# Attention and the first layer's early products in the program's order on every engine, with the state products first and the state in two copies

## The chip, the core and the metric

The kernel runs on one core of one Trainium2 chip. The metric is device time in microseconds of one execution. The engines are TensorE (PE, with its weight loads as PEld), VectorE (DVE), ScalarE (ACT), GpSimd (POOL) and SyncE (SP), whose queue issues all transfers here. The kernel is built by a framework whose scheduler chooses the order of instructions on each engine from a simulated timeline, unless the program says otherwise; on the chip each engine then takes its instructions in that order.

## The reference

A retention layer (linear attention with a decay per head), then two dense feed-forward layers:

```python
for t in range(S):                       # S = 768, batch 2, 8 heads of 64
    state = gamma * state + einsum('bhd,bhe->bhde', k[:, :, t], v[:, :, t])
    y[:, :, t] = scale * einsum('bhd,bhde->bhe', q[:, :, t], state)
x = y as 1536 tokens of 512 features
g = mish(x @ w_in); x = g @ w_out                                  # d_ff 2048
x = (sigmoid(x @ w_gate) * (x @ w_val)) @ w_out2                   # d_ff 1536
```

## The kernel before

**Attention.** The 1536 tokens are 12 chunks of 128, six for each batch. For a chunk j, `at_scores` (line 432) makes the scores of all heads (tile `sc`, 8 matmuls on 64 rows of the array), POOL scales the values (`vp`) and, for the first chunks, prepares a scale table (`og`), and DVE masks the scores into `a`. `at_out` (line 450) adds up the chunk's output in tile `ao`: 8 matmuls of `a` with `vp` on 128 rows (line 457) and, except in the first chunk of a batch, 8 of the state with the queries on 64 rows (line 465). DVE scales it into `acc`. `at_state` (line 473) adds the chunk's keys and values to the state in PSUM (tile `st`, 8 matmuls on 128 rows, line 482), and ACT copies it into the one tile `s_t`, from which the next chunk's `at_out` reads. A chunk thus has four groups of 8 matmuls: scores, output, state read (I call it inter) and state.

**Transfers.** Each chunk loads two blocks of 512 KB (`qk_t`, `nv_t`, three buffers each). The weights come in pieces of 512 KB as 64-bit numbers (`raw`, three buffers) and are decoded to fp32: ACT (line 77, `v`), three DVE steps (lines 78 to 80), then `put` splits the result into a high part (ACT, line 67) and a low part (DVE, line 68) in `w`. `pump` (line 176) starts one such step of the weights.

**Dense products beside attention.** All dense products are three matmuls of 512 columns (hh, hl, lh), made by `mm3`. While attention runs, eight pieces of the first layer, each of 12 matmuls into one bank `h`, are made beside chunks 4 to 11 (line 519 and line 522): four for tokens 0 to 511, from `xc` (the split of `acc` by `put_plain` after chunk 3), and four for tokens 512 to 1023, from `B11` and `B21` (the split after chunk 7). ACT makes `e` (Mish) from each bank and `g`'s high part, POOL `g`'s low part. `blocks` (line 492) writes for each chunk j: scores of chunk j+1, one dense piece, output and state of chunk j, loads of chunk j+3.

**Order.** Scores, output, state and loads stand under `tc.high_priority()`; apart from that the scheduler chooses freely, so it mixes groups of matmuls, decode steps and transfers as its timeline sees fit.

**After attention.** `out1_first(0)` (line 535) begins the long dense part of 2244 matmuls, in which PE is the engine that sets the pace up to the end.

## Time and profile before

| | |
|---|---|
| median of 3 runs | 619.88 us (617.69 to 619.91) |
| the profiled execution's own time | 619.43 us |
| its span (first to last instruction) | 617.6 us |
| PE busy | 605.4 us (98%) |
| DVE, POOL, ACT busy | 412.5, 314.2, 250.3 us |
| `qk_t`, `nv_t`: issue to landing, median | 4.7, 5.5 us |
| `raw` of the first layer: issue to landing, median | 3.7 and 3.8 us |

PE is busy nearly all the time by this count, but a matmul that waits in the array for a change of shape counts as busy, so the busy share does not say how much of the time is work. The shares of the chain of waits and the duration of groups of matmuls say more. Attention and the eight dense pieces beside it end at about 95 us; the rest of the span is the dense part.

### The profile page before, as it was taken

Reading aid. Unit: us, or ns where it says so; the run is one execution under the profiler, and the core shown is the slowest. Engines: PE = TensorE matmul, PEld = TensorE weight load, DVE = VectorE, ACT = ScalarE, POOL = GpSimd, SP = SyncE. Lnnn points to the kernel's source line nnn. Section 1 sums busy time; section 2 is a strip of 40 time slices with the busy share of each in tenths; the row PEclk is TensorE's granted clock in tenths of the full one; section 3 lists DMA queues with packets and bytes.
Section 4 is the critical chain, followed back from the end, with each engine's and each line's share of the span. In section 5 each row is a group of like instructions: output and inputs, shape, how many; then the busy total and the mean of one; then the engine's idle time right before and its main releaser. Section 6 shows DMA issues by size and latency. Waiting matters only on the chain.

```text
span 617.6 us, 7968 instructions
## 1 busy us (share of the span) xinstructions
PE 605.4 (98%) x3056; PEld 488.7 (79%) x3056; DVE 412.5 (67%) x572; ACT 250.3 (41%) x433; POOL 314.2 (51%) x263
## 2 busy tenths in 40 slices
PE   8999999999999999998999999999999999999997
PEld 6767778888878788886788777888888888888885
DVE  3998339604795848647676996778477587573454
ACT  2535135624635444433443555543244244333210
POOL 5222333513968658546660556757378367466200
PEclk9999999999999999999999999999999999999999
DMA  9985301300321304121012012213112122100014
GB/s 342 370 319 169 120 2 36 102 2 34 103 88 50 136 1 137 52 85 68 34 36 69 0 64 73 70 68 102 34 69 68 69 68 76 61 1 1 1 51 154
DMA packets 15591, 52.27 MB, mean 85 GB/s; under 512 B 1984, under 2 KB 2112, under 8 KB 15552
## 3 DMA queue, kind: packets, MB, share of 16 engines
q1 hardware_dynamic: 15552, 51.75, 24.2%
q8 instruction: 24, 0.39, 0.3%
q14 instruction: 15, 0.12, 0.1%
HBM read 48.60 MB, written 3.15 MB: 84 GB/s over the span
## 4 chain that ended last, share of the span: by engine, by line
PE 76%; DVE 16%; POOL 3%; issue 2%; ACT 2%; DMA 1%; SPq 0%; DVEq 0%; ACTq 0%; POOLq 0%
PE h L86 31%; PE o L86 30%; PE hx L86 7%; DVE v L79 4%; DVE v L80 3%; DVE v L78 2%; PE ao L457 2%; PE sc L438 2%; DVE acc L324 2%; PE ao L465 2%; POOL w L68 1%; POOL g L68 1%; POOL og L444 1%; DVE T L68 1%; PE st L482 1%
## 5 line engine op out<-in xcount | busy, mean ns | idle before, releaser
L68 POOL TENSOR_TENSOR g<-e,g 128x512 fp32r<-128x512 f32 x80 | 115.0, 1445 | 120.9 <-ACT g L67 120.9
L86 PE MATMUL o<-g,w 128*128 128x512 f32 x576 | 141.3, 394 | 2.9 <-DVE acc L324 2.7
L86 PEld LDWEIGHTS o<-g,w 128*128 128x128 f32 x576 | 108.6, 190 | 28.2 <-DVE acc L324 5.0
L86 PE MATMUL h<-T,w 128*128 128x512 f32 x444 | 112.2, 390 | 1.0 <-DVE T L68 0.6
L68 POOL TENSOR_TENSOR w<-v,w 128x512 fp32r<-128x512 f32 x56 | 76.2, 1369 | 67.7 <-ACT w L67 67.5
L86 PE MATMUL o<-w,g 128*128 128x512 f32 x432 | 106.0, 389 | 0.0
L86 PE MATMUL h<-B,w 128*128 128x512 f32 x384 | 100.3, 391 | 0.8 <-DVE e L314 0.8
L86 PEld LDWEIGHTS h<-T,w 128*128 128x128 f32 x444 | 83.2, 188 | 19.4 <-DVE T L68 1.0
L86 PEld LDWEIGHTS o<-w,g 128*128 128x128 f32 x432 | 81.0, 188 | 17.1 <-POOL g L68 0.4
L86 PEld LDWEIGHTS h<-B,w 128*128 128x128 f32 x384 | 71.6, 188 | 16.7 <-DVE e L314 1.3
L324 DVE TENSOR_TENSOR acc<-o,acc 128x512 f32<-128x512 f32 x72 | 49.0, 685 | 39.0 <-PE o L86 38.7
L67 ACT ACTIVATE g<-e 128x512 fp32r<-128x512 f32 x84 | 52.5, 630 | 53.2 <-DVE e L314 35.1
L67 ACT ACTIVATE w<-v 128x512 fp32r<-128x512 f32 x68 | 42.4, 630 | 72.3 <-DVE v L80 44.4
L77 ACT ACTIVATE v<-raw 128x512 f32<-128x512 f32 x68 | 45.2, 670 | 57.8 <-POOL w L68 20.0
L86 PE MATMUL h<-xc,w 128*128 128x512 f32 x264 | 67.6, 393 | 0.1
L78 DVE TENSOR_SCALAR v<-v 128x512 int32<-128x512 int32 x68 | 51.1, 752 | 24.5 <-ACT v L77 24.2
L79 DVE SCALAR_TENSOR_TENSOR v<-raw,v 128x512 int32<-128x512 int32 x68 | 64.9, 955 | 1.3
L68 POOL TENSOR_TENSOR w<-s,w 128x512 fp32r<-128x512 f32 x34 | 48.2, 1425 | 34.4 <-ACT w L67 34.0
L80 DVE SCALAR_TENSOR_TENSOR v<-raw,v 128x512 int32<-128x512 int32 x68 | 64.4, 947 | 0.6
L344 DVE TENSOR_TENSOR acc<-o,acc 128x512 f32<-128x512 f32 x60 | 41.1, 686 | 30.8 <-PE o L86 30.4
L86 PEld LDWEIGHTS h<-xc,w 128*128 128x128 f32 x264 | 49.1, 188 | 11.1 <-DVE xc L68 0.8
L86 PE MATMUL hx<-xc,w 128*128 128x512 f32 x216 | 55.6, 389 | 0.0
(62 smaller groups left out, 551.1 us busy)
## 6 DMA issues: line engine op xcount, KB each, us to landing
raw<-w1i SPq DMA_DIRECT2D x16, 512.0 KB, 3.7
raw<-w1o SPq DMA_DIRECT2D x16, 512.0 KB, 3.8
qk_t<-qk SPq DMA_DIRECT2D x12, 512.0 KB, 4.7
nv_t<-nv SPq DMA_DIRECT2D x12, 512.0 KB, 5.5
raw<-w2g SPq DMA_DIRECT2D x12, 512.0 KB, 3.2
raw<-w2v SPq DMA_DIRECT2D x12, 512.0 KB, 3.4
raw<-w2o SPq DMA_DIRECT2D x12, 512.0 KB, 3.4
out<-acc SPq DMA_DIRECT2D x12, 256.0 KB, 2.0
```

What stands on the lines that cost most here:

```text
L67: nc.scalar.activation(out=hi, in_=raw, func=AF.Copy)
L68: eng.tensor_tensor(out=lo, in0=raw, in1=hi.bitcast(F32), op=ALU.subtract)
L77: nc.scalar.activation(out=v, in_=high.bitcast(F32), func=AF.Copy, scale=2.0 ** -112)
L78: nc.vector.tensor_scalar(out=b, in0=b, scalar1=3, scalar2=None, op0=ALU.logical_shift_left)
L79: nc.vector.scalar_tensor_tensor(out=b, in0=low, scalar=29, in1=b, op0=ALU.logical_shift_right, op1=ALU.bitwise_or)
L80: nc.vector.scalar_tensor_tensor(out=b, in0=high, scalar=SIGN, in1=b, op0=ALU.bitwise_and, op1=ALU.bitwise_or)
L86: nc.tensor.matmul(out=o, lhsT=w(a), rhs=x(b), start=first and n == 0, stop=last and n == 2, skip_group_check=more)
L324: nc.vector.tensor_tensor(out=acc, in0=o, in1=acc, op=ALU.add)
L344: nc.vector.tensor_tensor(out=acc, in0=o, in1=acc, op=ALU.add)
L438: nc.tensor.matmul(out=sc[e][:, p, :], lhsT=t[r, 1, p, :], rhs=t[r, 0, p, :])
L457: nc.tensor.matmul(out=o[D * e:D * e + D, p, :], lhsT=v[:, 2 * p + e, :], rhs=a[:, e, p, :], start=p == 0, stop=p == NP - 1 and not inter, ...
L465: nc.tensor.matmul(out=o[r, p, :], lhsT=s_t[r, p, :], rhs=t[r, 0, p, :], start=False, stop=p == NP - 1, skip_group_check=True,)
```

## The change

A wrapper `InOrder` stands in front of each engine and the transfer queue. As long as the list `early` is not empty (up to the end of attention), each instruction that is issued through it is told to stand after the one issued before it on the same engine, so the scheduler must keep the program's order there. After attention `early.clear()` gives the choice back. With that the program's own order is rewritten: `fin` makes the state products before the output; a chunk's output, state, loads and one piece of weights stand ahead of its dense piece; the low part of a weight (`late`) is issued one step later than its high part; weights are loaded one per chunk, two ahead of the first chunk where there were three; and the state gets a tile of its own per chunk from a pool with two buffers, where it was one tile.

```diff
+    class InOrder:
+        def __init__(self, engine):
+            self.engine, self.last = engine, None
+        def __getattr__(self, name):
+            call = getattr(self.engine, name)
+            if not early:
+                return call
+            def ordered(**kw):
+                with tc.issue_after(self.last) if self.last else nullcontext():
+                    i = call(**kw)
+                self.last = i.ins
+                return i
+            return ordered
+    pe, dve, act, pool, sync = [InOrder(e) for e in (nc.tensor, nc.vector, nc.scalar, nc.gpsimd, nc.sync)]
...
     def put(key, v):
         t = slot(key)
-        split(v, t[:, 0], t[:, 1], lo_eng["w"])
+        hi, lo = t[:, 0], t[:, 1]
+        act.activation(out=hi, in_=v, func=AF.Copy)
+        late.append(lambda: lo_eng["w"].tensor_tensor(out=lo, in0=v, in1=hi.bitcast(F32), op=ALU.subtract))
+        if not early:
+            late.pop(0)()
...
     def pump(n=1):
+        while late:
+            late.pop(0)()
...
-            nc.scalar.activation(out=s_t, in_=st, func=AF.Copy)
+            s_t[j + 1] = at.tile([P, NP, D], F32, tag="s", name="s")
+            act.activation(out=s_t[j + 1], in_=st, func=AF.Copy)
 
         def fin(j):
+            at_state(j)
             at_out(j)
-            at_state(j)
 
         def blocks(j0, dense):
 
             for j in range(j0, j0 + SPC):
                 if j + 1 < NSUB:
-                    with tc.high_priority():
-                        at_scores(j + 1)
+                    at_scores(j + 1)
+                fin(j)
+                load(j + 3)
+                load_piece()
                 if dense:
                     dense.pop(0)()
-                with tc.high_priority():
-                    fin(j)
-                    load(j + 3)
+                if j < SPC:
+                    pump()
             run(dense)
```

On PE, one chunk with a dense piece before (chunk 5, the chunk after it gives the scores; L438 is scores, L457 output, L465 inter, L86 dense):

```order
L438 MATMUL sc<-qk_t 128x128 x3
L457 MATMUL ao<-a,vp 64x128
L438 MATMUL sc<-qk_t 128x128 x2
L457 MATMUL ao<-a,vp 64x128 x4
L438 MATMUL sc<-qk_t 128x128
L457 MATMUL ao<-a,vp 64x128
L438 MATMUL sc<-qk_t 128x128
L457 MATMUL ao<-a,vp 64x128
L438 MATMUL sc<-qk_t 128x128
L457 MATMUL ao<-a,vp 64x128
L465 MATMUL ao<-qk_t,s_t 64x128 x8
L86 MATMUL h<-xc,w 128x512 x12
```

and such a chunk now, on the same engine (chunk 7; every early instruction has the wrapper's line):

```order
L65 MATMUL sc<-qk_t 128x128 x8
L65 MATMUL st<-vp,nv_t 64x64 x8
L65 MATMUL ao<-a,vp 64x128 x8
L65 MATMUL ao<-qk_t,s 64x128 x8
L65 MATMUL h<-xc,w 128x512 x12
```

The matmuls of two groups that alternated one by one now stand in groups of 8, and the state products stand second.

On DVE, where chunk 3 ends and `xc` is made, before (L447 masks scores, L469 scales the output, L78 to L80 decode):

```order
L447 TENSOR_TENSOR a<-sc,ma 128x512 x2
L80 SCALAR_TENSOR_TENSOR v<-raw,v 128x512
L469 TENSOR_TENSOR acc_87<-ao,og_108 128x4x128
L78 TENSOR_SCALAR v<-v 128x512
L68 TENSOR_TENSOR w<-v,w 128x512
L79 SCALAR_TENSOR_TENSOR v<-raw,v 128x512
L68 TENSOR_TENSOR xc<-acc_87,xc 128x512 x2
L80 SCALAR_TENSOR_TENSOR v<-raw,v 128x512
L68 TENSOR_TENSOR xc<-acc_87,xc 128x512
```

and at the same place on DVE now:

```order
L65 TENSOR_TENSOR a<-sc,ma 128x512 x2
L65 TENSOR_TENSOR acc_87<-ao,og_108 128x4x128
L65 TENSOR_TENSOR w<-v,w 128x512
L65 TENSOR_SCALAR v<-v 128x512
L65 SCALAR_TENSOR_TENSOR v<-raw,v 128x512 x2
L65 TENSOR_TENSOR xc<-acc_87,xc 128x512 x4
L65 TENSOR_TENSOR a<-sc,ma 128x512 x2
```

The whole decode of the fourth piece now stands ahead of the first `xc`, and all four `xc` stand ahead of the next masking.

On ACT, where chunk 7 ends and `B11` and `B21` (here B_84 and B_85) are made, before:

```order
L77 ACTIVATE v<-raw 128x512 x2
L486 ACTIVATE s_t<-st 128x256
L67 ACTIVATE B_84<-acc_88 128x512 x2
L67 ACTIVATE B_85<-acc_88 128x512 x2
L308 ACTIVATE e<-h 128x512
L67 ACTIVATE w<-v 128x512
L67 ACTIVATE g<-e 128x512
```

and now:

```order
L65 ACTIVATE s<-st 128x256
L65 ACTIVATE e<-h 128x512
L65 ACTIVATE g<-e 128x512
L65 ACTIVATE v<-raw 128x512
L65 ACTIVATE w<-v 128x512
L65 ACTIVATE B_84<-acc_88 128x512 x2
L65 ACTIVATE B_85<-acc_88 128x512 x2
```

The four splits now stand behind the Mish of the dense piece just made, and behind a whole decode. From `out1_first` on, the order on PE is the same in both but for one group of six matmuls.

## Rows read from the trace of the kernel before

**Rows 1.** The page, part 4: shares of the chain that ended last.
```profile
PE 76%; DVE 16%; POOL 3%; issue 2%; ACT 2%; DMA 1%; SPq 0%; DVEq 0%; ACTq 0%; POOLq 0%
```

**Rows 2.** Table by stretch: length, busy us (instructions) of each engine, clock, DMA.
```profile
7.30:30.30 23.00, 21.10 (x308) 16.99 (x306) 20.18 (x33) 9.66 (x18) 10.46 (x10) 1.00 0.99 385
...
95.00:617.00 522.00, 513.63 (x2245) 421.11 (x2243) 350.68 (x477) 217.04 (x372) 283.12 (x233) 1.00 0.18 61
```

**Rows 3.** The same for 30.30 to 94.80, by tile: sc, ao, st, h.
```profile
30.30:94.80 64.50, 16.02 (x96) 10.87 (x96) 9.46 (x14) 1.00 0.43 149
...
30.30:94.80 64.50, 24.32 (x208) 14.08 (x208) 5.48 (x8) 1.00 0.43 149
...
30.30:94.80 64.50, 5.68 (x84) 3.92 (x80) 2.28 (x6) 1.00 0.43 149
...
30.30:94.80 64.50, 24.82 (x96) 17.16 (x96) 0.00 (x0) 3.54 (x6) 1.00 0.43 149
```

**Rows 4.** Chain of waits in order of time: start, us, piece (two records a matmul).
```profile
44.10 0.41 PE sc L438 x2
44.52 0.36 PE ao L457 x2
...
57.09 2.96 PE h L86 x12
...
81.44 1.09 PE sc L438 x16
82.53 1.02 PE ao L465 x16
83.55 0.61 PE st L482 x16
```

**Rows 5.** Timeline, ACT and DVE in the first chunks: start, us, what, [idle before].
```profile
13.20 0.69 ACT L77 ACTIVATE v<-raw 128x512 f32<-128x512 f32 x1 [4.03 <-DMA raw<-w1i]
...
17.65 0.42 DVE L78 TENSOR_SCALAR v<-v 128x512 int32<-128x512 int32 x1
17.99 0.68 DVE L68 TENSOR_TENSOR w<-v,w 128x512 fp32r<-128x512 f32 x1
...
18.59 0.68 DVE L80 SCALAR_TENSOR_TENSOR v<-raw,v 128x512 int32<-128x512 int32 x1
...
19.80 1.28 DVE L447 TENSOR_TENSOR a<-sc,ma 128x512 f32<-128x512 f32 x2
...
20.99 0.68 DVE L80 SCALAR_TENSOR_TENSOR v<-raw,v 128x512 int32<-128x512 int32 x1
```

**Rows 6.** Timeline: POOL and DVE at the same time.
```profile
23.60 1.11 POOL L440 TENSOR_TENSOR vp<-nv_t,ck 128x512 f32<-128x512 f32 x1 [2.79 <-DMA nv_t<-nv]
23.85 1.41 DVE L79 SCALAR_TENSOR_TENSOR v<-raw,v 128x512 int32<-128x512 int32 x1
```

**Rows 7.** Timeline: the first split, the first dense piece, the first of out1_first.
```profile
27.71 2.18 ACT L67 ACTIVATE xc<-acc 128x512 fp32r<-128x512 f32 x4
...
30.33 3.14 PE L86 MATMUL h<-xc,w 128*128 128x512 f32 x10
...
95.00 5.60 PE L86 MATMUL o<-g,w 128*128 128x512 f32 x24
```

**Rows 8.** Timeline: the split of a bank, high part on ACT and low part on POOL.
```profile
81.93 0.63 ACT L67 ACTIVATE g<-e 128x512 fp32r<-128x512 f32 x1
82.63 1.27 POOL L68 TENSOR_TENSOR g<-e,g 128x512 fp32r<-128x512 f32 x1 [4.22 <-ACT g L67]
```

**Rows 9.** Two waits of PE, and the clock by stretch around the second.
```profile
18.37 1.16 PE L438 MATMUL sc<-qk_t 64*128 64x128 f32 x16 [1.47 <-DMA qk_t<-qk]
...
290.56 9.74 PE L86 MATMUL o<-g,w 128*128 128x512 f32 x35 [2.29 <-DVE acc L324]
...
290.40:293.80 3.40, 3.24 (x8) 2.56 (x9) 0.98 (x3) 0.90 (x2) 0.85 (x1) 0.50 0.41 146
```

**Rows 10.** The page, part 6: a chunk's second block from issue to landing.
```profile
nv_t<-nv SPq DMA_DIRECT2D x12, 512.0 KB, 5.5
```

More of the change, by code (lines that the diff above doesn't have):

```diff
@@ L1 @@
-from contextlib import ExitStack
+from contextlib import ExitStack, nullcontext
 import numpy as np
@@ L75, in decode @@
         b = v.bitcast(I32)
-        nc.scalar.activation(out=v, in_=high.bitcast(F32), func=AF.Copy, scale=2.0 ** -112)
-        nc.vector.tensor_scalar(out=b, in0=b, scalar1=3, scalar2=None, op0=ALU.logical_shift_left)
-        nc.vector.scalar_tensor_tensor(out=b, in0=low, scalar=29, in1=b, op0=ALU.logical_shift_right, op1=ALU.bitwise_or)
-        nc.vector.scalar_tensor_tensor(out=b, in0=high, scalar=SIGN, in1=b, op0=ALU.bitwise_and, op1=ALU.bitwise_or)
+        act.activation(out=v, in_=high.bitcast(F32), func=AF.Copy, scale=2.0 ** -112)
+        dve.tensor_scalar(out=b, in0=b, scalar1=3, scalar2=None, op0=ALU.logical_shift_left)
+        dve.scalar_tensor_tensor(out=b, in0=low, scalar=29, in1=b, op0=ALU.logical_shift_right, op1=ALU.bitwise_or)
+        dve.scalar_tensor_tensor(out=b, in0=high, scalar=SIGN, in1=b, op0=ALU.bitwise_and, op1=ALU.bitwise_or)
         return v
@@ L85, in mm3 @@
         for n, (a, b) in enumerate(((0, 0), (0, 1), (1, 0))):
-            nc.tensor.matmul(out=o, lhsT=w(a), rhs=x(b), start=first and n == 0, stop=last and n == 2,
+            pe.matmul(out=o, lhsT=w(a), rhs=x(b), start=first and n == 0, stop=last and n == 2,
                              skip_group_check=more)
@@ L103 @@
     cnt = {"dma": 0, "raw": 0, "task": 0}
-    steps, sums_t, vs = [], {}, {}
-    lo_eng = {"w": nc.vector, "g": nc.gpsimd}
+    steps, late, sums_t, vs = [], [], {}, {}
+    lo_eng = {"w": dve, "g": pool}
     def load_piece():
@@ L112, in load_piece @@
         t = stg.tile([P, DM], I64, tag="raw", name="raw")
-        nc.sync.dma_start(out=t, in_=src[kind][i])
+        sync.dma_start(out=t, in_=src[kind][i])
         raws.append(t)
@@ L121, in next_raw @@
         cnt["raw"] += 1
-        while cnt["dma"] < min(len(pieces), cnt["raw"] + STG):
+        while not early and cnt["dma"] < min(len(pieces), cnt["raw"] + STG):
             load_piece()
@@ L188, in weight @@
             steps.pop(0)[1]()
+        while late:
+            late.pop(0)()
         return w_t[key]
@@ L222, in put_t4 @@
         for k in range(2):
-            split(ts[2 + k], b_t["T4"][:, k, 0], b_t["T4"][:, k, 1], nc.vector)
+            split(ts[2 + k], b_t["T4"][:, k, 0], b_t["T4"][:, k, 1], dve)
     g_t = {}
@@ L247, in p1 @@
             r["s1"] = up.tile([P, N], F32, tag="u", name="s1")
-            nc.scalar.activation(out=r["s1"], in_=r["b1"], func=AF.Copy)
+            act.activation(out=r["s1"], in_=r["b1"], func=AF.Copy)
         def p6():
@@ L270, in c22 @@
         def c22():
-            nc.vector.tensor_tensor(out=r["b2"], in0=r["bB"], in1=r["u3"], op=ALU.add)
+            dve.tensor_tensor(out=r["b2"], in0=r["bB"], in1=r["u3"], op=ALU.add)
         def p2():
@@ L307, in mish @@
         e = ep.tile([P, N], F32, tag="e", name="e")
-        nc.scalar.activation(out=e, in_=h, func=AF.Mish)
+        act.activation(out=e, in_=h, func=AF.Mish)
         put_g(e, key)
@@ L323, in o1 @@
         acc = acc_t[c][:, d, :]
-        nc.vector.tensor_tensor(out=acc, in0=o, in1=acc, op=ALU.add)
+        dve.tensor_tensor(out=acc, in0=o, in1=acc, op=ALU.add)
     def o1_first(c, d):
@@ L437, in at_scores @@
                     r = slice(D * e, D * e + D)
-                    nc.tensor.matmul(out=sc[e][:, p, :], lhsT=t[r, 1, p, :], rhs=t[r, 0, p, :])
+                    pe.matmul(out=sc[e][:, p, :], lhsT=t[r, 1, p, :], rhs=t[r, 0, p, :])
             vp_t[j] = at.tile([P, 2 * NP, D], F32, tag="vp", name="vp")
-            nc.gpsimd.tensor_tensor(
+            pool.tensor_tensor(
                 out=vp_t[j], in0=nv_t[j][:, 1], in1=ck[:, j % SPB].to_broadcast([P, 2 * NP, D]), op=ALU.mult
@@ L456, in at_out @@
                 for e in range(2):
-                    nc.tensor.matmul(
+                    pe.matmul(
                         out=o[D * e:D * e + D, p, :], lhsT=v[:, 2 * p + e, :], rhs=a[:, e, p, :],
@@ L464, in at_out @@
                         r = slice(D * e, D * e + D)
-                        nc.tensor.matmul(
-                            out=o[r, p, :], lhsT=s_t[r, p, :], rhs=t[r, 0, p, :], start=False, stop=p == NP - 1,
+                        pe.matmul(
+                            out=o[r, p, :], lhsT=s[r, p, :], rhs=t[r, 0, p, :], start=False, stop=p == NP - 1,
                             skip_group_check=True,
                         )
-            nc.vector.tensor_tensor(
+            dve.tensor_tensor(
                 out=acc_t[j // SPC][:, :, j % SPC * P:j % SPC * P + P], in0=o, in1=og[j % SPB], op=ALU.mult
@@ L481, in at_state @@
                 for e in range(2):
-                    nc.tensor.matmul(
+                    pe.matmul(
                         out=st[D * e:D * e + D, p, :], lhsT=k[:, 0, 2 * p + e, :], rhs=v[:, 2 * p + e, :],
@@ L515 @@
         load_piece()
+        load_piece()
         at_scores(0)
-        blocks(0, seq([lambda: None] * SPC))
+        blocks(0, [])
         put_plain()
```

73 lines of the change are left out of this document (37 added, 36 removed).

## The prediction

> **What bounds the kernel now.** I read the chain of waits by engine first: PE holds 76% of it and DVE 16% [rows 1]. Then the table by stretch. From 95 us to the end PE is busy 513.6 of 522 us [rows 2], and by the order PE does there what it did before, so whatever is gained or lost ahead of `out1_first` is handed on to the end. Its first matmul starts at 95.00 us [rows 7]; this is the time to forecast. Ahead of it lie two stretches. Up to about 30 us DVE is busy 20.2 of 23 us [rows 2]: it masks, scales and decodes, and the first dense piece, which waits for the split `xc`, starts at 30.33 [rows 7]. From there to 95 us the chain runs through PE alone, and the reader should look at how long a group of 8 matmuls takes there. Where scores and outputs alternate, a matmul of the one takes 0.41 us and one of the other 0.36; in one piece 8 scores take 1.09 us, 8 matmuls of `ao` 1.02, 8 of the state 0.61, and a dense piece of 12 with the change of shape behind it 2.96 [rows 4]. So 16 alternating matmuls cost 8 x 0.77 = 6.2 us against 2.1 in two groups: each change between 64 and 128 rows stops the array.
>
> **The change, part by part.**
>
> *Grouping.* By records (two a matmul for the fp32 groups), the stretch from the first dense piece to `out1_first` holds 96/16 = 6 groups of scores, 208/16 = 13 of output and inter, 80/16 = 5 of state (by the weight loads; some matmul records are doubtful) and 96/12 = 8 dense pieces [rows 3]. In the new order the same work stands behind the start of the first dense piece: scores of chunks 6 to 11, output of 5 to 11, inter of 5 and 7 to 11, state of 6 to 10. In groups it costs 6 x 1.09 + 13 x 1.02 + 5 x 0.61 + 8 x 2.96 = 6.5 + 13.3 + 3.1 + 23.7 = 46.5 us, where it took 95.00 - 30.33 = 64.7. **Gain: 18.1 us**, less what waits are new.
>
> *The start of the first dense piece.* Now DVE takes everything in the program's order: the decode of pieces 0 to 3 whole, maskings of chunks 2 to 4, outputs 1 to 3, low parts 0 to 2, then `xc`. It can begin when piece 0 has landed, and ACT's copy of it, at 13.20, ends at 13.9 [rows 5]; the queue carries the same bytes ahead of it. From the starts in rows 5, a decode takes 0.34 + 2 x 0.60 = 1.55, a pair of maskings 1.19, any other step 0.60. So 13.9 + 4 x 1.55 + 3 x 1.19 + 6 x 0.60 = 27.3; then ACT's high part of piece 3 (0.63) and of the first `xc` (2.18/4 = 0.55 [rows 7]): 28.5 at best. Against that, a DVE step that begins while POOL works can be held: a decode step of 0.68 took 1.41 and ended after POOL's `vp` [rows 5, 6]. POOL has `vp` and `og` in each of these chunks, so I bound it by 4 x 0.73 = 2.9: 31.4. I take 30.4, above the middle because handovers between engines are not counted: 0.1 later than now. Ends: -1.8 and +1.1. Cover: transfers. One weight piece less stands ahead of chunk 3's blocks, so the wait of 1.47 us for them [rows 9] should not grow.
>
> *The first dense piece itself.* Its twelve matmuls want the four parts of `xc` one after the other. ACT gives a high part each 0.55 us, DVE a low part each 0.60, so it takes about 0.4 us more than its own time. PE stands idle ahead of it: chunk 4's groups end when its masking (about 25 us in the same reckoning) is two groups old, near 27.5. The idle stretch is 2 to 3 us. Such a wait is in the trace: after 2.29 us PE ran 3.40 us at 0.50, that is 1.2 GHz instead of 2.4, and after 1.47 us it stayed at full clock [rows 2, 9]. Half of 3.4 us is 1.7 at most, and part of it falls on time in which PE would wait for `xc` anyway: I take 0.8 for both, between 0.4 and 2.1.
>
> The Trainium skill ("TensorE: Matmul & The Clock Gate", section "HAM oscillation — how this bites in real kernels") says that waits between bursts of matmuls bring the half rate back, burst after burst. By that rule a strict order, in which PE stands still more often but for shorter times, speaks against this change; by the rows only this wait is as long as the one that was followed by half clock, and the sum has 0.8 us for it. What the rule would make of all chunks is the third rival.
>
> *The second handover, at chunk 8.* `B11` and `B21` now stand on ACT behind the Mish of the piece just made, its split, and a whole decode. From the end of that piece: two ACT steps of 0.63 [rows 8], the copy 0.69 and the decode 1.55 [rows 5], the high part 0.63, then high parts at 0.55 each and a low part: the last at 4.1 + 4 x 0.55 + 0.68 = 7.0 us. PE meanwhile has scores, state, output and inter (1.09 + 0.61 + 2 x 1.02 = 3.7) and nine of its twelve matmuls (about 2.1), and would want that part at 5.9. So +1.1 at least; with two DVE steps held by POOL +2.6. I take 1.9.
>
> *The other chunks.* Here the new order could close a loop: masking of chunk j+2 stands on DVE behind the decode in chunk j, which is behind ACT's copy, which is behind the Mish of dense piece j. From the end of piece j this is 0.63 + 0.63 + 0.69 + 1.55 + 1.19 = 4.7 us; with POOL's low part and `vp` (1.27 and 1.11 [rows 6, 8]) both in the way 7.1. PE wants the masking one chunk and two groups later: 1.09 + 0.61 + 2 x 1.02 + 2.96, then 1.09 + 0.61, in all 8.4. Slack 1.3 to 3.7: nothing is lost. If the cover fails, I bound it by 0.3 in each of six chunks, 1.8. State first: the copy of the state has a chunk to be made, and with two tiles it no longer waits for the readers; it was not on the chain in groups, so I put it at nothing. Transfers: a chunk's blocks are issued after its buffer's last reader, 5.5 us before they land [rows 10], and are wanted a dense piece and a chunk later (2.96 + 6.7 us): hidden by 4 us. The queue holds a weight piece behind them and waits for the decode of the chunk before, which is over by then.
>
> *After attention* the order is kept, the waits there hang on PE, and everything moves by the same amount: 0. What is late next is the split of chunk 11's output, wanted 5.4 us after `out1_first` starts; DVE has about twelve steps of 0.60 from the end of inter 11, 2.7 us ahead: just in time.
>
> *Sum.* 18.1 - 0.1 - 0.8 - 1.9 = 15.3 us. `out1_first` at 79.7, and against the profiled execution's 619.43 us: **604.1 us**. That execution stands 0.45 below the median of the runs, which changes nothing.
>
> **The rivals.**
>
> *The handovers eat half of it.* Everything at its far end: start +1.1, first piece 2.1, second handover 2.6 and a half clock behind it 1.7, chunks 1.8: 9.3 of the 18.1 us, gain 8.8, 610.6 us. For it: DVE is nearly full up to 30 us. Against it: several independent terms must all go wrong.
>
> *The change does not do what it says.* If the long alternating stretches were long because a matmul waited for data, and not for the change of rows, grouping would only move the waits: 619.5 us. For it: nothing but that PE's busy time hides waits. Against it: the same groups take 1.09, 1.02 and 0.61 us when they stand alone [rows 4].
>
> *Slower: the loop of the order closes.* If a piece of weights lands late, ACT stands at its copy, DVE at its decode, and the masking and so PE behind both, in every chunk; before, the scheduler could put the masking ahead. From 3.7 us of delay on PE waits. If PE waited 2.3 us in each of the seven chunks and ran 3.4 us at half clock each time, as at 290 us [rows 9], a chunk would cost 2.3 + 1.7 = 4.0 more, 28 us in all: 632 us. It turns slower from 15.3/7 = 2.2 us a chunk. Against it: pieces are issued two chunks ahead, some 13 us. The page of the skill named above stands on this rival's side.
>
> **How the numbers follow.** My forecast (600.5 to 608) has 0.72; handovers that eat half (608 to 613) 0.14; no effect 0.05; slower 0.06; and 0.03 for a gain beyond 19 us, were the first dense piece 1.8 us earlier and nothing else lost. A range from 600.5 to 611 leaves out no more than 2 in 10. A measurement of this kernel tells about 0.5%, 3.1 us, from no change. Faster by more: 0.72 + 0.14 + 0.03 less a little, 0.88; within it 0.06; slower 0.06.
>
> **What would show it.** Right: in the new chain of waits every group of scores stands in one piece of about 1.1 us, `out1_first` starts near 80 us, PE waits for `xc` near 28 us and for `B11` at chunk 8, nowhere else over 1 us up to the end. The gain in the span equals that of `out1_first`. Wrong: PE waits for maskings (DVE) in chunks 5 to 11, granted clock at 0.50 between 40 and 75 us, groups of 16 records that take 2 us or more, or a dense part that is longer than the 522 us it took.

## The result: 609.6 us, and the profile after

The changed kernel takes 609.6 us in the median of 4 runs (609.13 to 611.22), the kernel before 619.26 us beside it: a ratio of 0.9852, with an interval of 0.9824 to 0.9881, so it is faster by 1.5%. The forecast was 604.1 us with a range from 600.5 to 611. The time lies inside the range, but at its slow end: by the prediction's own bands it belongs to the rival in which the handovers eat half of the gain (608 to 613, worked out as 610.6 us, chance 0.14) and not to the forecast (600.5 to 608, chance 0.72). The profiled execution took 610.06 us, with a span of 608.3.

`out1_first` now starts at 85.60 us, where it was 95.00 [rows 7]: 9.4 us earlier. The span is 9.3 us shorter. What was gained ahead of `out1_first` is handed on whole, as expected.

The table by stretch: length, busy us (instructions) of PE, PEld, DVE, ACT, POOL, then the granted clock. First three short stretches after waits, then the dense rest:

```profile
18.20:21.60 3.40, 3.40 (x40) 3.07 (x40) 3.33 (x5) 1.03 (x3) 3.04 (x2) 0.50 0.90 355
35.30:38.70 3.40, 3.40 (x13) 2.36 (x13) 2.86 (x5) 0.60 (x2) 0.00 (x0) 0.50 0.48 188
62.60:66.00 3.40, 3.14 (x7) 2.21 (x8) 3.16 (x6) 2.04 (x5) 0.00 (x0) 0.50 0.83 334
86.00:608.00 522.00, 513.37 (x2243) 420.73 (x2242) 354.48 (x482) 218.97 (x376) 292.78 (x233) 1.00 0.19 62
```

The last row is the twin of the second of [rows 2]: 513.4 busy of 522 us, where it was 513.6. From the first matmul of `out1_first` to the end it is 522.7 us, where it was 522.6. The first three are new: three times ahead of 86 us TensorE ran 3.4 us at 0.50, that is 1.2 GHz instead of 2.4. The kernel before had none there.

The same table by tile, from the first dense piece to `out1_first`, as in [rows 3] (sc, ao, h; PE first, then PEld):

```profile
33.29:85.70 52.41, 7.30 (x96) 6.15 (x96) 8.96 (x14) 0.93 0.48 169
...
33.29:85.70 52.41, 13.69 (x208) 11.25 (x208) 5.44 (x8) 0.93 0.48 169
...
33.29:85.70 52.41, 27.20 (x96) 19.01 (x96) 0.00 (x0) 4.17 (x7) 0.93 0.48 169
```

The counts are those of before, so the same work stands behind the first dense piece. The six groups of scores keep PE busy for 7.3 us instead of 16.0, the thirteen of output and inter 13.7 instead of 24.3. The dense pieces went up, from 24.8 to 27.2, because two of them run at half clock for the most part.

One chunk in the chain of waits (start, us, piece), the twin of [rows 4]:

```profile
49.97 1.09 PE sc L65 x16
51.06 0.61 PE st L65 x16
51.68 1.90 PE ao L65 x32
53.58 2.96 PE h L65 x12
```

Four whole groups, 6.56 us a chunk, and no wait between them.

The first handover in the timeline (start, us, engine, what, [idle before <- releaser]):

```profile
17.08 1.16 PE L65 MATMUL sc<-qk_t 64*128 64x128 f32 x16 [2.92 <-DMA qk_t<-qk]
...
23.20 1.49 POOL L65 TENSOR_TENSOR og<-og,sg 128x512 f32<-128x512 f32 x1
23.71 1.26 DVE L65 TENSOR_SCALAR v<-v 128x512 int32<-128x512 int32 x1
...
27.37 1.16 PE L65 MATMUL sc<-qk_t 64*128 64x128 f32 x16 [1.43 <-DMA qk_t<-qk]
...
28.77 1.29 POOL L65 TENSOR_TENSOR vp<-nv_t,ck 128x512 f32<-128x512 f32 x1 [4.08 <-DMA nv_t<-nv]
29.19 2.86 DVE L65 SCALAR_TENSOR_TENSOR v<-raw,v 128x512 int32<-128x512 int32 x2
30.02 1.48 POOL L65 TENSOR_TENSOR og<-og,sg 128x512 f32<-128x512 f32 x1
...
33.29 0.50 PE L65 MATMUL h<-xc,w 128*128 128x512 f32 x1 [2.24 <-ACT xc L65]
34.01 4.02 PE L65 MATMUL h<-xc,w 128*128 128x512 f32 x11 [0.23 <-DVE xc L65]
37.96 1.49 PE L65 MATMUL sc<-qk_t 64*128 64x128 f32 x16
```

The first dense piece starts at 33.29 us (before 30.33, [rows 7]) and is over at 37.96, after 4.67 us instead of 2.96. Two DVE decode steps that stand beside POOL's `vp` and `og` take 2.86 us instead of 1.42, one step 1.26 instead of 0.42. In the kernel before POOL had made all five `og` in one go, from 7.06 to 12.09 us, ahead of the decodes; the strict order puts one of them into each chunk, beside a decode.

The second handover, at chunk 8:

```profile
58.43 1.03 DVE L65 TENSOR_SCALAR v<-v 128x512 int32<-128x512 int32 x1 [0.49 <-ACT v L65]
59.49 2.14 DVE L65 SCALAR_TENSOR_TENSOR v<-raw,v 128x512 int32<-128x512 int32 x2
62.20 2.17 ACT L65 ACTIVATE B<-acc 128x512 fp32r<-128x512 f32 x4
62.86 4.63 PE L65 MATMUL h<-B,w 128*128 128x512 f32 x12 [2.74 <-ACT B L65]
...
67.43 1.16 PE L65 MATMUL sc<-qk_t 64*128 64x128 f32 x16
```

PE waits 2.74 us for `B11`, whose split stands on ACT behind a decode that takes DVE 3.2 us (58.43 to 61.63) beside POOL's steps, and the piece then runs at half clock, 4.63 us long. The chunk takes 10.97 us (scores at 56.45 and again at 67.42) instead of 6.56: 4.4 us lost.

### The profile page after: what moved, and what is told of

Its sections match the earlier page's. It is cut to its first block, busy times and chain, and to the rows that moved or that the text cites. A ratio compares the mean times of both kernels' runs of the same rounds, so it can differ in the third digit from the quotient of the medians.

```text
span 608.3 us, 7961 instructions
## 1 busy us (share of the span) xinstructions
PE 587.5 (97%) x3056; PEld 480.6 (79%) x3056; DVE 420.3 (69%) x572; ACT 249.8 (41%) x433; POOL 325.2 (53%) x263
## 4 chain that ended last, share of the span: by engine, by line
PE 74%; DVE 16%; DMA 2%; ACT 2%; POOL 2%; issue 2%; SPq 0%; DVEq 0%; ACTq 0%
PE o L108 31%; PE h L108 28%; PE hx L108 7%; PE h L65 4%; DVE v L101 3%; PE ao L65 2%; DVE v L102 2%; DVE v L100 2%; DVE acc L354 2%; DMA qk_t<-qk 2%; DVE v L65 1%; PE sc L65 1%; POOL w L162 1%; POOL g L90 1%; DVE T L90 1%
## 5 line engine op out<-in xcount | busy, mean ns | idle before, releaser
L90 POOL TENSOR_TENSOR g<-e,g 128x512 fp32r<-128x512 f32 x72 | 103.1, 1441 | 83.4 <-ACT g L89 83.4
L108 PE MATMUL h<-B,w 128*128 128x512 f32 x336 | 87.8, 390 | 0.8 <-DVE e L344 0.8
L108 PEld LDWEIGHTS h<-B,w 128*128 128x128 f32 x336 | 62.9, 188 | 14.4 <-DVE e L344 1.2
L89 ACT ACTIVATE g<-e 128x512 fp32r<-128x512 f32 x76 | 47.6, 631 | 52.6 <-DVE e L344 35.1
L161 ACT ACTIVATE w<-v 128x512 fp32r<-128x512 f32 x58 | 36.1, 630 | 62.6 <-DVE v L102 34.7
L100 DVE TENSOR_SCALAR v<-v 128x512 int32<-128x512 int32 x58 | 44.4, 767 | 23.2 <-ACT v L99 22.9
L99 ACT ACTIVATE v<-raw 128x512 f32<-128x512 f32 x58 | 38.6, 670 | 49.7 <-POOL w L162 20.0
L102 DVE SCALAR_TENSOR_TENSOR v<-raw,v 128x512 int32<-128x512 int32 x58 | 57.0, 984 | 0.5
L101 DVE SCALAR_TENSOR_TENSOR v<-raw,v 128x512 int32<-128x512 int32 x58 | 56.4, 973 | 1.1
L108 PE MATMUL h<-xc,w 128*128 128x512 f32 x216 | 54.8, 389 | 0.0
L108 PEld LDWEIGHTS hx<-xc,w 128*128 128x128 f32 x216 | 40.6, 188 | 8.4
```

The source lines that it names most:

```text
L89: act.activation(out=hi, in_=raw, func=AF.Copy)
L90: eng.tensor_tensor(out=lo, in0=raw, in1=hi.bitcast(F32), op=ALU.subtract)
L99: act.activation(out=v, in_=high.bitcast(F32), func=AF.Copy, scale=2.0 ** -112)
L100: dve.tensor_scalar(out=b, in0=b, scalar1=3, scalar2=None, op0=ALU.logical_shift_left)
L101: dve.scalar_tensor_tensor(out=b, in0=low, scalar=29, in1=b, op0=ALU.logical_shift_right, op1=ALU.bitwise_or)
L102: dve.scalar_tensor_tensor(out=b, in0=high, scalar=SIGN, in1=b, op0=ALU.bitwise_and, op1=ALU.bitwise_or)
```

## The experiments

The theory, once the result was known: the groups of matmuls bring what the sum said, and the shortfall sits in the two handovers, in new waits of PE and in the half clock that follows them. The rivals: the groups alone are worth less; or the loss is spread over all chunks; or another part of the change (the forced order, the state in two copies) costs it. Each ratio is against the kernel before, run in turn with it on the same chip; its medians there were 618.1 to 618.9 us.

| kernel | median us | ratio [interval] | first dense piece | out1_first |
|---|---|---|---|---|
| the change | 609.6 | 0.9852 [0.9824, 0.9881] | 33.29 | 85.60 |
| alternating groups | 636.0 | 1.0261 [1.0204, 1.0319] | 39.76 | 111.08 |
| no order forced | 606.0 | 0.9789 [0.9768, 0.9810] | 31.64 | 82.03 |
| before, without priorities | 611.4 | 0.9884 [0.9869, 0.9898] | 28.67 | 87.47 |
| order forced on PE alone | 614.2 | 0.9927 [0.9908, 0.9945] | 40.13 | 90.01 |
| on PE and the transfer queue | 606.6 | 0.9805 [0.9783, 0.9827] | 36.12 | 83.46 |
| state as before | 609.8 | 0.9851 [0.9832, 0.9869] | 33.58 | 85.13 |
| splits first | 605.6 | 0.9798 [0.9773, 0.9822] | 30.77 | 80.71 |
| splits first, no decode behind | 601.3 | 0.9705 [0.9678, 0.9732] | 31.01 | 76.67 |
| `og` first | 608.1 | 0.9819 [0.9795, 0.9843] | 32.88 | 83.63 |
| idle matmuls in the waits | 607.1 | 0.9817 [0.9782, 0.9851] | 36.72 | 85.90 |
| both splits and `og` first | 599.7 | 0.9689 [0.9669, 0.9709] | 34.77 | 80.44 |
| the same with idle matmuls | 598.0 | 0.9680 [0.9655, 0.9706] | 29.55 | 75.20 |

The last two columns come from each kernel's one profiled execution. For several kernels that was the longest of their runs; it is far from the median for the idle matmuls (610.36 us) and for both splits and `og` first (604.8 us), and 1.0 us from it for splits first with no decode behind (602.35 us).

### The grouping undone

```diff
-                    at_scores(j + 1)
+                    at_scores(j + 1, out_begin(j) if j >= SPC else None)
```

Here each score matmul is followed by one output matmul of the chunk before, from chunk 4 on (`out_begin` returns the function that makes one). All else of the change stays, the forced order too.

> The changed kernel, with one thing undone: in chunks 4 to 10 the 8 scores of the next chunk and the 8 output matmuls (128 rows) of this chunk alternate one by one again, in a forced order on PE. Theory (changes between 64 and 128 rows cost the time): 7 chunks x (6.2 - 2.0) = 29 us more PE time; a part of it falls into the waits at the two handovers (some 5 us), so about 634 us, slower than the kernel before. Rival (the groups were long because matmuls waited for data): no more than 1 us a chunk, about 610 us.

It took 636.0 us, 2 us above the theory's value, and slower than the kernel before. The total is in part luck, since PE also ran 13.7 us at half clock in it, which the theory did not have. The price is therefore read from dense pieces at full clock. In its chain of waits, chunk 6 begins with the first two rows and ends with a dense piece; the next dense piece is the last row:

```profile
54.01 0.42 PE sc L65 x2
54.42 0.36 PE ao L65 x2
...
60.69 2.94 PE h L65 x12
...
71.34 2.95 PE h L65 x12
```

A pair of matmuls takes 0.78 us, where the same pair in groups takes (1.09 + 1.02)/8 = 0.26. From piece to piece it is 10.65 us against 6.56: 4.1 a chunk, which is what 8 x (0.78 - 0.26) gives. That grouping is worth its price is shown by this run. It also shows that the strict order by itself, with alternating groups, is a loss.

That it is the change of rows, and not the alternation as such, can be seen in the kernel before, where outputs and state products alternate at 15 us (both 128 rows) and state reads and state products at 36 us (64 and 128 rows):

```profile
15.36 0.28 PE L457 MATMUL ao<-a,vp 128*64 128x128 f32 x1
...
15.81 0.86 PE L457 MATMUL ao<-a,vp 128*64 128x128 f32 x12
...
36.28 0.43 PE L465 MATMUL ao<-qk_t,s_t 64*64 64x128 f32 x2
36.64 0.33 PE L482 MATMUL st<-vp,nv_t 128*64 128x64 f32 x2
```

From the start of the first row to that of the second there are four records of outputs and six of states. They take 0.45 us, and would take 4 x 1.02/16 + 6 x 0.61/16 = 0.48 in whole groups: nothing is lost. A pair of the other kind takes 0.36 + 0.26 = 0.62 us against (1.02 + 0.61)/8 = 0.20 in groups. The Trainium skill (TensorEngine Tiling (Array Packing), section "Key Properties") says that a change of tiling mode drains the array. The traces agree with it and give the price, about 0.26 us for each of the two changes in a pair of scores and outputs; the drain itself no row shows.

### The forced order and the priorities

No order forced: the wrapper is taken away, the program's new order stays as a wish to the scheduler.

```diff
-    pe, dve, act, pool, sync = [InOrder(e) for e in (nc.tensor, nc.vector, nc.scalar, nc.gpsimd, nc.sync)]
+    pe, dve, act, pool, sync = nc.tensor, nc.vector, nc.scalar, nc.gpsimd, nc.sync
```

> The changed program text without the forced order: no instruction is told to stand after another, so the scheduler chooses on all engines; there is no high priority any more. By the order its groups on PE stay nearly whole, and xc and B are split as the scheduler likes. Theory (whole groups bring the gain, the forced order on ACT and DVE costs the handovers): out1_first near 79 us, about 603 us. Rival (the forced order itself brings the gain): near 619 us.

606.0 us, 3 us slower than the theory had it, and far from the rival. The scheduler by itself keeps the groups nearly whole once the high priorities are gone. At the second handover PE takes the piece in parts and waits 0.26, 0.98 and 0.17 us. So the force isn't what brings the gain; it costs some 3 us (the two intervals do not overlap).

The kernel before with nothing changed but the priorities:

```diff
-                    with tc.high_priority():
-                        at_scores(j + 1)
+                    at_scores(j + 1)
...
-                with tc.high_priority():
-                    fin(j)
-                    load(j + 3)
+                fin(j)
+                load(j + 3)
```

> The kernel before, with only the three high priorities of scores, output, state and loads taken away; nothing is forced. By its order on PE the groups then stand nearly whole, but some weight pieces stand ahead of chunk loads on the transfer queue. Theory (the high priority made the scheduler mix the groups, and the mixing alone costs the time): groups of about 1.1 and 1.9 us in the chain, no alternation, faster than before, 605 to 612, less the waits for qk_t that the queue brings. Rival (the gain needs the forced order): 617 to 621.

611.4 us, 1.2% faster than before. The timeline of PE where the second handover is (and a stretch of the table with the clock below it):

```profile
52.34 1.16 PE L438 MATMUL sc<-qk_t 64*128 64x128 f32 x16
...
57.42 0.65 PE L465 MATMUL ao<-qk_t,s_t 64*64 64x128 f32 x6 [2.90 <-ACT s_t L486]
59.68 0.79 PE L86 MATMUL h<-B,w 128*128 128x512 f32 x1 [1.61 <-ACT B L67]
```

```profile
58.10:68.30 10.20, 8.62 (x42) 5.73 (x44) 5.16 (x9) 2.57 (x5) 1.04 (x1) 0.50 0.86 298
```

The scores ahead of the handover (1.16 us) and the outputs behind them (1.09) are whole groups, and the time goes to waits for ACT instead, 2.90 for the one state tile and 1.61 for `B11`, with 10.2 us at half clock from 58.1 on. That the high priorities caused the mixing of scores and outputs is shown for this scheduler: without them these no longer alternate. Two dense pieces are still cut up among the small groups.

The order forced on PE alone, and then on PE and the transfer queue:

```diff
-    pe, dve, act, pool, sync = [InOrder(e) for e in (nc.tensor, nc.vector, nc.scalar, nc.gpsimd, nc.sync)]
+    pe = InOrder(nc.tensor)
+    dve, act, pool, sync = nc.vector, nc.scalar, nc.gpsimd, nc.sync
```

> The changed kernel with the forced order on PE alone; ACT, DVE, POOL and the transfer queue are the scheduler's. Theory (of the 6 us by which the gain fell short, most is the order on ACT and DVE at the two handovers): out1_first near 80 us, about 604 us. Rival (the shortfall is PE's own order, which stands still before the first piece of each four): about 610 us as with the change.

Both theories missed: 614.2 us. The timeline shows why, on the transfer queue (SPq, the block for chunk 5) and on PE:

```profile
26.48 0.38 SPq L453 DMA_DIRECT2D qk_t<-qk  x1
...
31.57 2.08 PE L65 MATMUL sc<-qk_t 64*128 64x128 f32 x16 [5.84 <-DMA qk_t<-qk]
```

The queue, now free, takes four pieces of weights (from 16.44 to 26.06 us) ahead of the queries and keys of chunk 5, which are issued at 26.48. PE, now bound to its order, waits 5.84 us for them. Two stretches of 6.8 us at half clock go with it, from 30.4 and from 40.6 us. The second handover costs nothing here, so the loss is another one than in the changed kernel. The next kernel is to show that it is the queue:

```diff
-    dve, act, pool, sync = nc.vector, nc.scalar, nc.gpsimd, nc.sync
+    pe, sync = InOrder(nc.tensor), InOrder(nc.sync)
+    dve, act, pool = nc.vector, nc.scalar, nc.gpsimd
```

> The order is forced on PE and on the transfer queue alone; DVE, ACT and POOL are the scheduler's. Theory (pe_only lost its time to the order of the transfers: chunk blocks behind weight pieces, 5.8 us of waiting for qk_t): no wait of PE for qk_t over 3 us, first dense piece at 30 to 33 instead of 40, out1_first at 79 to 83, 603 to 607. Rival (pe_only lost it to the free order on DVE and ACT): first dense piece still near 40, about 614.

606.6 us, as the theory said; no wait for `qk_t` is over 1.8 us. `out1_first` is 0.5 us behind the forecast's end, and the first dense piece came much later than its 30 to 33, at 36.12, because of a wait that I had not thought of:

```profile
30.10 1.12 PE L65 MATMUL st<-vp,nv_t 128*64 128x64 f32 x16 [3.15 <-issue]
```

By the times, the state products wait until ACT has copied the state of the chunk before (29.64 to 30.01 us), and that copy stands on ACT behind a weight's split. The second handover again costs nothing. Against the changed kernel this leaves DVE, ACT and POOL to the scheduler, and by the medians it is 3 us faster (the intervals just overlap): strict order on those three brings nothing.

### The state products first, the state in two copies

```diff
-            s_t[j + 1] = at.tile([P, NP, D], F32, tag="s", name="s")
+            s_t[j + 1] = ac.tile([P, NP, D], F32, tag="s", name="s")
...
-            at_state(j)
             at_out(j)
+            at_state(j)
```

> The changed kernel with the state part undone: output and inter first, then the state products, and the state in one tile, in the same forced order. Theory (state first and two copies are worth nothing where groups stay whole): within 1 us of the change, 609.6 us. Rival (the next chunk's inter waits for the copy, or the copy for the last inter): 0.5 to 1 us a chunk, 614 to 619 us.

609.8 us, ratio 0.9851 against 0.9852: as forecast, this part is worth nothing under the forced order. In the kernel without priorities PE did wait for the one state tile; that wait was not tried with two.

### The handovers taken away

Splits first: `xc` and `B11`, `B21` are made right behind the output that they split, ahead of the decode.

```diff
-        def blocks(j0, dense):
+        def blocks(j0, dense, split=None):
...
                 fin(j)
+                if split and j == j0 + SPC - 1:
+                    split()
...
-        blocks(0, [])
-        put_plain()
-        blocks(SPC, plain1(0) + plain1(1))
-        put_block("B11", 1, 0)
-        put_block("B21", 1, 2)
+        blocks(0, [], put_plain)
+        blocks(SPC, plain1(0) + plain1(1), put_b)
```

> The changed kernel with the splits xc and B11, B21 made right behind the output of chunks 3 and 7, ahead of the Mish, the decode and the loads of that chunk; all else in the forced order. Theory (both handovers are late because the splits stand behind a whole decode, and PE falls to half clock in the wait): first dense piece at about 31 instead of 33.3 us, no half clock in the two pieces, the second handover without a wait; 4.2 + 4.4 = 8.6 us less, 601.5 us. Rival (the splits are late because DVE is full, wherever they stand): within 2 us of the change, 608 to 610 us.

605.6 us, between the two. The first dense piece starts at 30.77 us, as forecast. Both handovers' waits and their stretches of half clock are gone (the one at 18 us is not), but two other waits appear in PE's timeline:

```profile
35.94 1.59 PE L65 MATMUL ao<-a,vp 128*64 128x128 f32 x16 [1.03 <-DVE a L65]
...
63.39 0.69 PE L65 MATMUL st<-vp,nv_t 128*64 128x64 f32 x16 [2.00 <-issue]
```

What came late before (the splits) is early now, and what stood behind the same decode is late: the masking of chunk 5, and the copy of a state. So at these two places the engines had no room for a decode at all. The next kernel leaves it out there; the weights have that much lead.

```diff
+                if split and j == 2 * SPC - 1:
+                    quiet.append(1)
                 if dense:
                     dense.pop(0)()
-                if j < SPC:
+                    quiet.clear()
+                if j < SPC - 1:
                     pump()
```

(`quiet` stops the `pump` that stands inside a dense piece.)

> The kernel with the splits right behind the outputs of chunks 3 and 7, and besides no weight piece decoded in these two chunks (each later piece moves one chunk on; all ten are still decoded in time). Splits first alone left 1.0 us of wait for a masking in chunk 5, and 2.0 us ahead of the state products of chunk 9. Theory (these waits are the decode and what stands behind it on DVE and ACT): both gone, out1_first near 77.5 instead of 80.7 us, 602 us. Rival (the splits themselves take DVE's and ACT's time): no change, 605.6 us.

601.3 us, as forecast, 8 us faster than the change. PE's dense pieces at the second handover:

```profile
55.73 3.01 PE L66 MATMUL h<-B,w 128*128 128x512 f32 x12
62.28 3.01 PE L66 MATMUL h<-B,w 128*128 128x512 f32 x12
```

Chunk 8 takes 6.55 us, with no wait and no half clock: what it lost (4.4 us) is back whole, so it hung on the handover and not on the chunk. From the first dense piece to `out1_first` this kernel takes 76.67 - 31.01 = 45.66 us. The prediction's price list, with output and inter together at 1.90, gives 6 x 1.09 + 6 x 1.90 + 1.02 + 5 x 0.61 + 8 x 2.96 = 45.7: with the handovers out of the way the grouping brings what was worked out.

### POOL beside DVE, and the clock, by themselves

`og` first: POOL makes all five tables at chunk 1, so that only `vp` stands beside the decodes of chunks 2 to 4.

```diff
-            if 0 < j < SPB:
-                pool.tensor_tensor(out=og[j], in0=og[0], in1=sg[:, j].to_broadcast([P, NP, P]), op=ALU.mult)
+            for b in range(1, SPB) if j == 1 else ():
+                pool.tensor_tensor(out=og[b], in0=og[0], in1=sg[:, b].to_broadcast([P, NP, P]), op=ALU.mult)
```

> The changed kernel with all five scale tables og made by POOL one after the other beside chunk 1 (about 10 to 15 us), not one a chunk: POOL then has one step a chunk less up to chunk 4, where DVE's decode steps stood still behind it (1.26 for 0.42, 2.86 for 1.42 us). Theory (held DVE steps made the first dense piece late): it starts 1.0 to 1.5 us earlier than 33.3, about 608.3 us. Rival (the first stage is bound by the transfers and PE's waits for them): no change, 609.6 us.

608.1 us, as the theory said, but its interval overlaps with that of the change, so the time doesn't settle it. The first dense piece started at 32.88 us, 0.4 earlier and not 1.0 to 1.5. The profiled execution had 6.8 us at half clock from 17 us on, which hides part of it. The timeline of DVE shows another part:

```profile
14.72 2.86 DVE L65 SCALAR_TENSOR_TENSOR v<-raw,v 128x512 int32<-128x512 int32 x2
```

POOL's five tables, one after the other from 10.36 to 15.58 us, now hold the first decode, which takes 3.64 us from its start to the masking (13.86 to 17.50) where it took 1.83. The two decodes behind it take 1.79 and 1.78 us instead of 2.52 and 2.63, the fourth 2.65 instead of 3.31. So most of the hold was moved, and 0.4 us of it is gone.

Idle matmuls: five products into the bank of the piece, ahead of the first dense piece and of that at chunk 8. Their sum is cleared by the piece's first matmul.

```diff
+            for _ in range(FILL if i == 0 and key == (1, 0) and early else 0):
+                pe.matmul(out=o[:, 0:256], lhsT=filler[0][:, 0:P], rhs=filler[0])
```

> The changed kernel with five idle matmuls of 256 fp32 columns on PE ahead of the first and the fifth dense piece, into the bank that the piece then clears: PE works through the waits for xc and B, all else is as in the change. Theory (the half clock behind these waits doubles the time of the first matmuls of both pieces): no half clock near 35 and 62 us, the pieces take about 3 instead of 4.6 us, 3.0 us less in all, 606.6 us. Rival (the pieces are slow because the splits arrive one by one): about 609.6 us, or 1 to 2 us more where the idle matmuls stand in the way.

607.1 us, near the forecast, but again with an overlapping interval. In the profiled execution, the longest of the four, half clock fell elsewhere (6.8 us from 17 us on, 3.4 us from 30 us on, behind two waits for `qk_t`), so the first dense piece came at 36.72 and `out1_first` no earlier than in the change. Both pieces themselves ran at full clock. The second:

```profile
61.51 2.42 PE L67 MATMUL h<-z 128*128 128x256 f32 x10
64.32 0.49 PE L67 MATMUL h<-B,w 128*128 128x512 f32 x1 [0.39 <-ACT B L67]
65.04 2.78 PE L67 MATMUL h<-B,w 128*128 128x512 f32 x11 [0.23 <-DVE B L67]
```

PE works through the wait for `B11`, and the piece stays at full clock: 3.5 us with its wait for the low part, instead of 4.63. That the idle matmuls did this is not shown: with the state as before PE waited 2.58 us at the same place, without any, and the piece stayed at full clock too (63.35 to 66.83).

### Put together

Both splits early, no decode behind them, `og` first; and the same with six idle matmuls (into a bank that is cleared) in the wait for chunk 3's queries and keys.

```diff
+            for _ in range(6 if j == 3 else 0):
+                pe.matmul(out=sc[0].rearrange("p a b -> p (a b)")[:, 0:256], lhsT=filler[0][:, 0:P], rhs=filler[0])
```

> Both handovers split off early (as in split_skip), the og tables made at chunk 1 (as in og_first), and six idle matmuls on PE ahead of chunk 3's scores, where PE waited 2.9 us for qk_t and then ran 3.4 us at half clock. Theory (that half clock delays chunk 3's groups, with them the loads of the chunks behind and the first dense piece): no stretch at 0.50 near 18 us, first dense piece at 29.6 to 30.6 instead of 31.0, median 599.5 to 600.7. Rival (the first chunks are bound by the transfers and by DVE, PE's clock there is free): first piece at 31.0, 601.3 as split_skip.

> As best, without the six idle matmuls: both handovers split off early and the og tables made at chunk 1. It tells apart which of the two further edits took best from 601.3 to 598.0. If it was POOL (the og tables out of the way of the decode steps): half clock after the wait near 17 us is there again, but the first dense piece starts at 29.5 to 30.0 and the median is 597.7 to 599. If it was the clock (idle matmuls): the first dense piece starts at 30.7 to 31.2 and the median is 600.5 to 601.5. If each gave a part: between, 599 to 600.5.

598.0 us with the idle matmuls, 599.7 without: each edit gave a part, as far as medians tell; the intervals of the two overlap, and that of 599.7 overlaps with that of 601.3. With idle matmuls the kernel came out 1.5 us better than its theory (599.5 to 600.7), and its first dense piece, at 29.55 us, just ahead of the forecast. It is the best kernel of this study, 3.2% faster than before. Its timeline on DVE and PE, and the clock after the wait:

```profile
14.28 2.86 PE L67 MATMUL sc<-z 128*128 128x256 f32 x12
...
24.13 0.42 DVE L67 TENSOR_SCALAR v<-v 128x512 int32<-128x512 int32 x1
24.59 1.42 DVE L67 SCALAR_TENSOR_TENSOR v<-raw,v 128x512 int32<-128x512 int32 x2
```

```profile
18.20:21.60 3.40, 2.96 (x56) 2.62 (x56) 3.33 (x7) 0.95 (x3) 1.04 (x1) 1.00 0.92 363
```

With POOL out of the way the third decode's first step takes 0.42 us and its pair 1.42, where the changed kernel showed 1.26 and up to 2.86; the first decode is still held (3.65 us). There is no half clock in this execution from its start to its end. In each of the eight other profiled kernels with the order forced on every engine, which have no idle matmuls there, PE waited 2.6 to 3.1 us for chunk 3's queries and keys and half clock followed. Without the idle matmuls, one execution in six took 604.8 instead of about 599.6 us; its PE shows what a bad start costs:

```profile
16.99 2.08 PE L66 MATMUL sc<-qk_t 64*128 64x128 f32 x16 [2.81 <-DMA qk_t<-qk]
...
29.59 1.67 PE L66 MATMUL sc<-qk_t 64*128 64x128 f32 x16 [2.43 <-DMA qk_t<-qk]
```

After the first wait the clock is at half for 6.8 us, chunk 3 is late, its buffer comes free late, chunk 5's load is late, and PE waits a second time. With idle matmuls one execution of four was also longer (601.0 us), so they don't rule it out; its trace wasn't taken.

## Why the prediction was right, and where it was off

The forecast was that the gain comes from grouping alone, is lowered by the two handovers, and is handed on to the end. That is what the traces show. How much the handovers take was not foreseen: the time that came is the first rival's, and the range held because it reached into that rival's band. The prediction held against this rival that several independent terms must all go wrong. They were not independent: the price of a decode stands in both handovers, and so does half clock. Of the signs of being wrong that it names, one came: a granted clock of 0.50 between 40 and 75 us (62.6 to 66.0). The others, waits for maskings, groups of 2 us or more and a longer dense part, did not. Ahead of `xc` PE also waited over 1 us where the forecast saw nothing new, 2.92 and 1.43 us for queries and keys. The working, step by step, with 15.3 us forecast and 9.4 measured:

- **Grouping, 18.1 us: right.** Chunks without a handover took 6.56 us, a little less than reckoned, since inter follows output without a change in price (1.90 instead of 2.04 for the two). Six chunks with inter make that 0.8 us; 0.6 is what is left of the difference when the terms below are taken out. The kernel with alternating groups shows the reason directly: 4.1 us a chunk; the kernel with both handovers out of the way gives the sum of the groups to 0.1 us.
- **The start of the first dense piece, +0.1: wrong, +3.0, outside its bound of +1.1.** The step that failed is the price of DVE's decodes. In its timeline the four took 1.83, 2.52, 2.63 and 3.31 us, 4.1 us more than 4 x 1.55. Of this 1.1 us has nothing to do with POOL: a decode that nothing holds takes about 1.8 us (the first here, and 24.13 to 25.93 in the best kernel). I had read 0.34 us for its first step from a place where a step of other work follows [rows 5]; where the next step of a decode follows, it was 0.45 in the kernel before too:

```profile
16.59 0.42 DVE L78 TENSOR_SCALAR v<-v 128x512 int32<-128x512 int32 x1
17.04 0.69 DVE L79 SCALAR_TENSOR_TENSOR v<-raw,v 128x512 int32<-128x512 int32 x1
```

The other 3.0 us are POOL's holds. I had bounded them by 2.9, with one hold of 0.73 for each `vp`, and chose 1.9. The sum is near the bound, but made up otherwise: `og` holds decode steps too, and two POOL instructions in a row hold two or three of them. The rest of the shift is a wait of 0.72 for chunk 2's output, which PE made at half clock after it had waited 2.92 us for chunk 3's queries and keys. I had written that this wait should not grow from 1.47. The transfer was not late (those scores start at 17.08, before at 18.37); PE, with its groups whole, was ready earlier. The Trainium skill (SBUF — State Buffer, section "SBUF: two separate sides") says that DVE and POOL share a pair of ports, which one holds for a whole instruction. The trace agrees: a pair of steps took 2.86 us beside POOL and 1.42 alone, and with `og` made early the second and third decode got the 1.42 back, while the first lost about as much as they gained.

- **The first dense piece itself, 0.8: too little, about 2.0.** It took 4.67 instead of 2.96, and the scores behind it 1.42 instead of 1.09, because the clock was at half up to 38.7. The bound, 2.1, held.
- **The second handover, 1.9: too little, 4.4.** The wait was 2.74 (bound 2.6), and 1.7 of half clock came on top. The wait is the decode again, 3.2 us instead of 1.55. The 1.7 I had put into the rival only. The rows that I had spoke for more: a wait of 2.29 was followed by half clock, and my own bound for this wait reached beyond it. In the changed kernel 2.24, 2.74 and 2.92 us of waiting were followed by half clock, 1.11 and 1.43 were not. The length of a wait doesn't settle it, though: in other kernels waits of 2.44 (order on PE alone, at 18 us) and 2.58 us (state as before, at chunk 8) were not followed by it. The wait of 2.29 us in the dense part [rows 9] stands in the traces of the changed kernel (281 us) and of the best one too; behind it the changed kernel ran at half clock, the best one did not (start, us, piece, and a row of the table by stretch):

```profile
270.55 12.58 PE L110 MATMUL o<-g,w 128*128 128x512 f32 x54 [2.29 <-DVE acc L356]
...
272.00:274.00 2.00, 2.00 (x10) 1.63 (x10) 1.05 (x2) 1.22 (x3) 1.73 (x2) 1.00 0.01 4
```

What else decides it stays open.

- **The other chunks, 0: right.** No wait of PE between 40 us and the end of attention but the one at chunk 8. POOL was in the way of every decode (3.2 us instead of 1.8), and the loop from a piece's end to the end of the masking took 6.8 us (49.90 to 56.73), inside the 8.4 that PE gives it. The slower rival, in which this loop closes, did not come: half clock appeared only at the two handovers and at the third chunk.
- **State, and after attention, 0: right,** by the kernel with the old state, and by the dense rest, which took 522.7 us where it took 522.6.

In sum 0.6 - 2.9 - 1.2 - 2.5 = -6.0 us against the forecast's 15.3: 9.3. (The 0.6 is itself what was left over, so this sum is no test; the 45.7 us above are one.) The three sizes that were off have two causes: decodes that cost more, alone and beside POOL, than the rows had been read to say, and half clock behind three waits. The first was measured by the decode steps with and without POOL beside them. For the second the idle matmuls ahead of chunk 3 are the best evidence, from one profiled execution. That both handovers can be had for nothing is shown by the kernel with the splits first and no decode behind them.

The forecast's rule of the Trainium skill (TensorE: Matmul & The Clock Gate, section "HAM oscillation — how this bites in real kernels") gave more here than the sum gave it: half clock came back after three waits, of 2.24 to 2.92 us. It did not come in all chunks, as that rival wanted, because there were no waits there.

## What to carry to other kernels

Where small matmuls of different row counts alternate, group them first: a busy PE hides the price, and a comparison of a group's time alone and mixed shows it. Then look at what the strict order puts ahead of each handover between engines: whatever isn't needed for it (here a decode) costs PE a wait, and in these traces often half clock behind the wait. Price such a step from places where it stands as it will stand, with its own successor behind it and the other engines at work beside it. Forcing an order on the engines that feed PE brought nothing here; where PE's order is forced, the transfer queue's has to be forced with it (614 against 607 us), or PE waits for a load that the queue put last.

## What was not expected of the hardware

In the kernel with alternating groups TensorE stayed at half clock for 13.7 us, though PE counts as busy all through. The table by stretch:

```profile
28.30:42.00 13.70, 13.70 (x65) 9.46 (x64) 8.86 (x12) 3.10 (x6) 2.33 (x2) 0.50 0.33 118
```

It had waited 1.31 us ahead of that; the changed kernel waited 1.43 us at the same place, went on with whole groups, and kept its clock. While the small matmuls of alternating shape went on, from 28.3 to 36.4 us, the clock did not come back. They don't bring it down by themselves: the kernel before alternated in the same way at 1.00 (43 to 49 us). Why it fell, and why it came back at 42.0 us, isn't settled.

The spread between runs of one kernel goes with the granted clock: for the changed kernel 609.13 us at a mean of 0.992, 610.06 at 0.989 and 611.22 at 0.988. By an estimate from the 3.40 us stretches above, one of them more or less is 1.7 us.

POOL is held as well: `og` took 1.04 us alone and 1.48 beside DVE steps.
